# A linear-attention front and two feed-forward layers on one core: the order of small steps around the query tiles, the loads and the weight conversion is rewritten

## The chip, the cores and the metric

One Trainium2 chip, one core of it. The metric is the device time of one execution in microseconds (us); lower is better. Within the core the program uses TensorE (PE: matrix products and transposes), VectorE (DVE), ScalarE (ACT), GpSimd (POOL), and SyncE (SP), which issues all the transfers from one queue.

## The reference, cut to what matters

```python
def phi(x):                                   # x: q or k, scaled
    h = einsum('bhsd,md->bhsm', x, omega) - sum(x*x, -1)/2
    return exp(h - max(h, -1)) / sqrt(m)
kv  = einsum('bhsm,bhsd->bhmd', k_p, v)       # sums over the sequence
num = einsum('bhsm,bhmd->bhsd', q_p, kv)
den = einsum('bhsm,bhm->bhs', q_p, sum(k_p, 2)) + 1e-6
x = num / den                                 # 2304 tokens x 512
xn = x / sqrt(mean(x*x, -1) + 1e-6) * rms_g
y = (silu(xn @ w_gate) * (xn @ w_val)) @ w_out      # 512 -> 1536 -> 512
h = y @ w_in;  out = (h * cos(h)) @ w_out2          # 512 -> 2048 -> 512
```

Four sequences of 576 positions, 8 heads of 64, 128 features; everything is fp32.

## The kernel before, in words

The 2304 tokens are 18 tiles of 128. Each tile goes through the attention once as a key tile and once as a query tile. The code is issued in the order that is written (`manual_schedule`): every engine runs its own queue in that order, and an instruction that waits holds up all that stands behind it on its engine.

**Slots.** The front of the program is 23 slots (`SLOTS`). Each begins one tile: 18 key tiles, and query tiles 0 to 4 in slots 6, 9, 12, 15 and 22, because the sums of the first sequences are then finished. From slot 6 to slot 18 the pattern repeats every three slots: a query tile, a key tile, a key tile; the text calls this a triple. To begin a tile is `project` (16 products on PE into two PSUM banks, `kp_ps` or `qp_ps`) and `features` (on DVE the maximum over features, `kmx`/`qmx`; on ACT eight exponentials per tile, `ke`/`qe`). A key tile's product with v (`kv_product`) follows one slot later, for which the exponentials must be there.

**A query tile's later steps** (`query_step`) come in the slots after its own: 1 `transposed` and `keep_transposed` (PE transposes; the copies `eT` out of PSUM on DVE and ACT), 2 `sums` (PE, `num_ps`) and `quotients` (DVE), 3 `square` (ACT, sum of squares into `ms`), 4 `root` (`ms` times 1/512 plus epsilon on DVE, then the power -1/2 on POOL) and `norm` (DVE: x times `ms` times gain), 5 `turn` (PE transposes of x, `xT_ps`) and `put` 0 (ACT), 6 `put` 1 (DVE), and the store of a finished block of three tiles.

**Half steps.** The other 13 query tiles run beside the first feed-forward layer: each of its steps is two half steps, for gate and value (`gv_ps`, 12 products of 384 columns each), and a half step does the work of one slot: a new query tile every 2 or 3 half steps. After the product of a half step come the attention's steps and then half of the previous step's output product (`y_ps`, 6 products).

**PSUM.** There are four banks with the tag `w`, taken in turn by `kp_ps`, `qp_ps`, `xT_ps`, and, in the half steps, also by `gv_ps`, `eT_ps` and `num_ps`. A step that takes a bank waits until the step that had it four takings earlier has been read out.

**Weights.** Each of 68 chunks of weights (512 KB as raw fp64 bits) is loaded and turned into two fp32r halves: `W` on ACT, four integer operations on DVE (L153, L155, L157, L160), an add on POOL (L164), a cast on ACT (L170), a subtraction on POOL (L172). `tick(n)` issues the next n of these seven pieces. The load of chunk c+3 waits for the POOL add of chunk c, whose buffer it takes. In the slots `tick(4)` stands at the end of each until nine chunks are done.

**Loads.** `att.load` for the tile two slots ahead is the first thing in a slot (`AHEAD = 2`, three buffers). The v tile of three slots ahead is loaded right behind the `kv_product` that frees its buffer, and waits for it; key loads and weight loads stand in the same SP queue.

Of the kernel before, what the change touches and what calls it, by code (L numbers as in the profile page):

```python
# [38 lines left out]
AF = mybir.ActivationFunctionType  # L39
ALU = mybir.AluOpType  # L40
# [13 lines left out]
def attention_then_ffn(ctx: ExitStack, tc: tile.TileContext, qT, kT, v, omT, wc1, rms_g, wc2, out, B, H, S, D):  # L54
    nc = tc.nc
    M = omT.shape[1]
    DM = H * D
# [48 lines left out]
    quarter = const.tile([P, 1], F32, name="quarter")  # L106
    half_pi = const.tile([P, 1], F32, name="half_pi")
# [6 lines left out]
    class Weights:  # L114
# [26 lines left out]
        def run(self):  # L141

            last = len(self.todo)
            for c in range(3):
                self.load(c)
            yield
            self.exponent(0)
            yield
            for c in range(last + 1):
                if c < last:  # L150
                    w, raw = self.w.pop(c), self.raw.pop(c)
                    f = conv.tile([P, 512], I32, tag="f", name=f"f{c}", bufs=3)
                    nc.vector.tensor_scalar(f, w, 3, None, op0=ALU.logical_shift_left)  # L153
                    yield
                    nc.vector.scalar_tensor_tensor(f, w, SIGN, f, op0=ALU.bitwise_and, op1=ALU.bitwise_or)  # L155
                    yield
                    nc.vector.tensor_scalar(raw[:, :, 1], f, SIGN_AND_EXPONENT, None, op0=ALU.bitwise_and)  # L157
                    yield
                    rest = f32(raw[:, :, 1])
                    nc.vector.scalar_tensor_tensor(rest, raw[:, :, 0].bitcast(U32), 2.0 ** -52, rest,  # L160
                                                   op0=ALU.mult, op1=ALU.mult)
                    self.exponent(c + 1)
                    yield
                    nc.gpsimd.tensor_tensor(f32(f), f32(f), rest, op=ALU.add)  # L164
                    self.f[c] = f32(f)
                    yield
                    self.load(c + 3)
                if c > 0:
                    t = wpool.tile([P, 2, 512], F32R, tag="w", name=f"w{c - 1}")
                    nc.scalar.copy(t[:, 0], self.f[c - 1])  # L170
                    yield
                    nc.gpsimd.tensor_tensor(t[:, 1], self.f.pop(c - 1), f32(t[:, 0]), op=ALU.subtract)  # L172
                    self.out[self.todo[c - 1]] = t
                    self.done = c
                    yield
# [20 lines left out]
    wts = Weights()  # L196


    class Attention:
# [41 lines left out]
        def keep_transposed(self, t, r):  # L241
            ps = self.ps.pop(("eT", t, r))
            eT = self.tile_of("featT", [P, HP, P], F32, f"eT{t}_{r}")
            ps = ps.rearrange("p (h n) -> p h n", h=HP)
            if r or self.tag == "w":
                nc.scalar.copy(eT, ps)
            else:
                nc.vector.tensor_copy(eT, ps)
            self.eT[t, r] = eT
# [28 lines left out]

        def root(self, t):
            ms = self.ms[t]  # L280
            nc.vector.tensor_scalar(ms, ms, 1.0 / DM, 1e-6, op0=ALU.mult, op1=ALU.add)
            nc.gpsimd.tensor_tensor(ms, ms, minus_half, op=ALU.pow)

        def norm(self, t):
# [37 lines left out]
    with tc.manual_schedule():  # L322
        fp = ctx.enter_context(tc.tile_pool(name="fp", bufs=2, reuse_waits="tile"))
        early = ExitStack()
        ap = early.enter_context(tc.tile_pool(name="att", bufs=2, side="right", reuse_waits="tile"))
        depth = {"gain": 1, "raw": 3, "feat": 6, "mx": 6, "den": 4}
        kv = [ap.tile([P, KVW], F32, name=f"kv{b}", bufs=1) for b in range(B)]
        NV = 3
        vt = [ap.tile([P, H + 1, D], F32, name=f"v{i}", bufs=1) for i in range(NV)]
# [6 lines left out]
        def load_v(t):  # L336
            if t < NTILE:
                nc.sync.dma_start(vt[t % NV][:, 0:H], v[t])

        def kv_product(t, i):  # L340

            b, p0, n = parts(t)[i]
            end = p0 + n + t * P == (b + 1) * S
            for r in range(2):
                begin = (b, r) not in acc
                if begin:
                    acc[b, r] = bank("kv", f"kv_ps{b}_{r}")
                for h in range(HP):
                    hh = 2 * h + r
                    nc.tensor.matmul(  # L350
                        acc[b, r][:, h * P:(h + 1) * P], att.e["k", t, r][p0:p0 + n, h, :],
                        vt[t % NV][p0:p0 + n, hh::H - hh, :],
                        start=begin and h == 0, stop=end, skip_group_check=True)
                if end:
                    keep_kv(b, r)
            if i == len(parts(t)) - 1:
                for r in range(2):
                    del att.e["k", t, r]
                load_v(t + NV)

        def keep_kv(b, r):
            nc.vector.tensor_copy(
# [4 lines left out]
        def query_step(t, s):  # L367

            if s == 1:
                for r in range(2):  # L370
                    att.transposed(t, r)
                    att.keep_transposed(t, r)
            elif s == 2:
                for r in range(2):
                    att.sums(t, r)
                    att.quotients(t, r)
            elif s == 3:
                att.square(t)
            elif s == 4:
                att.root(t)  # L380
                att.norm(t)
            elif s == 5:
                att.turn(t)
                att.put(t, 0)
            elif s == 6:
                att.put(t, 1)
                if t % TPB == TPB - 1:
                    store(t // TPB, "x")
# [3 lines left out]
        tiles = {s: ("k", s) for s in range(6)}  # L392
# [3 lines left out]
        SLOTS = len(tiles)  # L396
# [3 lines left out]
        begins, then = {}, {}  # L400
        for s, (nm, t) in tiles.items():
            if nm == "k":
                for i in range(len(parts(t))):
                    then.setdefault(s + 1 + i, []).append((1, kv_product, t, i))
            else:
                for i in range(1, 7):
                    then.setdefault(s + i, []).append((-i, query_step, t, i))
        for todo in then.values():
            todo.sort(key=lambda e: e[0])
        AHEAD = 2  # L410
        order = sorted(tiles)

        def slot_before(s):

            at = order.index(s) if s in tiles else -1
            if at >= 0 and at + AHEAD < len(order):
                att.load(*tiles[order[at + AHEAD]])
            for k, f, *args in then.get(s, []):
                if k in (-6, -4):
                    f(*args)  # L420

        def slot_after(s):
            if s in tiles:
                att.project(*tiles[s])
                for r in range(2):
                    att.features(*tiles[s], r)
            for k, f, *args in then.get(s, []):
                if k not in (-6, -4):
                    f(*args)

        nc.sync.dma_start(om, omT)
        att.load(*tiles[0])
        att.load(*tiles[1])
        load_v(0)
        wts.tick(1)
        load_v(1)
        load_v(2)
        att.load_gain()
        for a in vt:
            nc.vector.memset(a[:, H], 1.0)  # L440
        for a in kv:
            nc.vector.memset(a[:, H * (D + 1):], 0.0)
        make_identity(nc, ident)
        nc.gpsimd.memset(quarter, 0.25)
        nc.gpsimd.memset(half_pi, math.pi / 2)
        nc.gpsimd.memset(minus_half, -0.5)
        nc.vector.tensor_scalar(om, om, SCALE, None, op0=ALU.mult)

        UP = 9
        for s in range(SLOTS):  # L450
            slot_before(s)
            slot_after(s)
            if wts.done < UP:
                wts.tick(4)


        att.tag = "w"
# [178 lines left out]
        for n, (g, blk, f, first, last) in enumerate(steps):  # L636
            in_g = len(GROUPS1[g]) * NBLK
            left = in_g - n % in_g - 3
            rate = rate_of(C1 * NF1 // 3 * (g + 2), left) if left > 0 else 0
            if g == 0 and n < G:  # L640
                rate = max(rate, 8)
            if n % in_g == 0:
                wts.freed = C1 * len(GROUPS1[0]) * g
            s = SLOTS + 2 * n
            slot_before(s)
            ps = product(blk, f, 0)
            a = silu(blk, f, ps)
            slot_after(s)
            if n >= 1:
                out1(*steps[n - 1][:3], hid[n - 1], *steps[n - 1][3:], (0, 1))  # L650
            wts.pace(rate / 2)
            flush(3)
            slot_before(s + 1)
            ps = product(blk, f, 1)
            hid[n] = gated(blk, f, a, ps)
            slot_after(s + 1)
            if n >= 1:
                out1(*steps[n - 1][:3], hid.pop(n - 1), *steps[n - 1][3:], (2, 3))
            if n in fetches:
                fetch(fetches[n], f"xhl{g}_{fetches[n]}")  # L660
            if g == 1 and f == GROUPS1[1][1]:
                take_back(blk)
            wts.pace(rate / 2)
            flush(3)
# [83 lines left out]
```

## Time and profile before

| | us |
|---|---|
| median of 3 runs (1034.16 to 1036.82) | 1035.8 |
| the profiled execution | 1034.51 |
| its span, first to last instruction | 1032.7 |
| PE busy in the span | 1001.7 (97%) |
| DVE busy | 630.3 (61%) |
| ACT busy | 474.8 (46%) |
| POOL busy | 191.9 (19%) |

PE is busy for 97% of the span, so what can be won is where it is not, and where it runs at its lower clock. A busy share over the whole span says nothing on a stage: the rows below are cut by stage. Times are from the start of the span. A line "[idle before <-releaser]" gives how long that engine had been idle ahead of the instruction and whose end ended it.

### The profile page before, as it was taken

Reading aid. Unit: us, or ns where it says so; the run is one execution under the profiler, and the core shown is the slowest. Engines: PE = TensorE matmul, PEld = TensorE weight load, DVE = VectorE, ACT = ScalarE, POOL = GpSimd, SP = SyncE. Lnnn points to the kernel's source line nnn. Section 1 sums busy time; section 2 is a strip of 40 time slices with the busy share of each in tenths; the row PEclk is TensorE's granted clock in tenths of the full one; section 3 lists DMA queues with packets and bytes.
Section 4 is the critical chain, followed back from the end, with each engine's and each line's share of the span. In section 5 each row is a group of like instructions: output and inputs, shape, how many; then the busy total and the mean of one; then the engine's idle time right before and its main releaser. Section 6 shows DMA issues by size and latency. Waiting matters only on the chain.

```text
span 1032.7 us, 15416 instructions
## 1 busy us (share of the span) xinstructions
PE 1001.7 (97%) x6040; PEld 948.0 (92%) x6040; DVE 630.3 (61%) x1180; ACT 474.8 (46%) x1018; POOL 191.9 (19%) x163
## 2 busy tenths in 40 slices
PE   7979899999999999999999999999999999999998
PEld 6878898998999999999999999878999999999997
DVE  5876575655524555324666337988667777566655
ACT  5766766856722222212333224555545444434443
POOL 1431222221101332102333001333112221000000
PEclk8998999999999999999999999999999999999999
DMA  7545142422221643502455412335202341003401
GB/s 247 205 153 175 63 159 77 163 94 81 112 93 50 246 153 126 190 1 88 160 181 209 158 62 82 123 134 192 82 21 103 121 179 67 2 1 123 153 31 61
DMA packets 32616, 121.90 MB, mean 118 GB/s; under 512 B 3616, under 2 KB 9888, under 8 KB 27936
## 3 DMA queue, kind: packets, MB, share of 16 engines
q1 hardware_dynamic: 32544, 120.93, 32.7%
q8 instruction: 47, 0.77, 0.3%
q14 instruction: 25, 0.20, 0.1%
HBM read 92.60 MB, written 28.31 MB: 117 GB/s over the span
## 4 chain that ended last, share of the span: by engine, by line
PE 72%; DVE 3%; ACT 1%; issue 0%; POOL 0%
PE gv_ps L462 8%; PE gv_ps L461 8%; PE gv_ps L463 8%; PE o_ps L463 6%; PE h_ps L463 6%; PE h_ps L461 6%; PE h_ps L462 6%; PE o_ps L462 6%; PE o_ps L461 6%; PE y_ps L461 4%; PE y_ps L462 4%; PE y_ps L463 4%; PE num_ps L258 1%; DVE o L574 1%; DVE turns L564 0%
## 5 line engine op out<-in xcount | busy, mean ns | idle before, releaser
L461 PE MATMUL gv_ps<-xhl,w 128*128 128x384 f32 x576 | 192.8, 335 | 1.8 <-DVE den L268 1.8
L463 PE MATMUL gv_ps<-xhl,w 128*128 128x384 f32 x576 | 192.6, 334 | 0.0
L462 PE MATMUL gv_ps<-xhl,w 128*128 128x384 f32 x576 | 192.4, 334 | 0.0
L164 POOL TENSOR_TENSOR f<-f,raw 128x512 f32<-128x512 f32 x68 | 90.2, 1326 | 530.9 <-issue 304.2
L463 PE MATMUL h_ps<-yhl,w 128*128 128x384 f32 x384 | 129.5, 337 | 0.0
L461 PE MATMUL h_ps<-yhl,w 128*128 128x384 f32 x384 | 129.3, 337 | 0.0
L462 PE MATMUL h_ps<-yhl,w 128*128 128x384 f32 x384 | 129.0, 336 | 0.0
L526 DVE TENSOR_TENSOR gv<-gv_ps,gv 128x384 f32<-128x384 f32 x72 | 40.1, 557 | 141.6 <-PE gv_ps L463 134.7
L527 ACT CAST t<-gv 128x384 fp32r<-128x384 f32 x72 | 37.0, 513 | 193.6 <-DVE gv L526 193.6
L463 PE MATMUL o_ps<-w,o 128*128 128x512 f32 x288 | 114.4, 397 | 0.6 <-DVE o L574 0.4
L462 PE MATMUL o_ps<-w,o 128*128 128x512 f32 x288 | 113.7, 395 | 0.0
L461 PE MATMUL o_ps<-w,o 128*128 128x512 f32 x288 | 112.4, 390 | 1.0 <-DVE osum L584 0.6
L569 ACT ACTIVATE turns<-turns,half_pi 128x384 f32<-128x384 f32 x96 | 59.3, 617 | 114.6 <-DVE turns L564 114.6
L461 PEld LDWEIGHTS gv_ps<-xhl,w 128*128 128x128 f32 x576 | 108.1, 188 | 2.4 <-issue 1.2
L462 PEld LDWEIGHTS gv_ps<-xhl,w 128*128 128x128 f32 x576 | 108.1, 188 | 0.0
L463 PEld LDWEIGHTS gv_ps<-xhl,w 128*128 128x128 f32 x576 | 108.1, 188 | 0.0
L172 POOL TENSOR_TENSOR w<-f,w 128x512 fp32r<-128x512 f32 x68 | 92.2, 1356 | 79.0 <-ACT w L170 49.2
L461 PE MATMUL y_ps<-t,w 128*128 128x384 f32 x288 | 99.5, 345 | 0.0
L463 PE MATMUL y_ps<-t,w 128*128 128x384 f32 x288 | 96.4, 335 | 0.0
L462 PE MATMUL y_ps<-t,w 128*128 128x384 f32 x288 | 96.4, 335 | 0.0
L574 DVE TENSOR_TENSOR o<-turns,o 128x384 fp32r<-128x384 f32 x96 | 61.4, 639 | 47.0 <-ACT o L572 47.0
L572 ACT CAST o<-turns 128x384 fp32r<-128x384 f32 x96 | 49.3, 514 | 75.5 <-DVE turns L571 74.5
(72 smaller groups left out, 1771.7 us busy)
## 6 DMA issues: line engine op xcount, KB each, us to landing
raw<-wc SPq DMA_DIRECT2D x68, 512.0 KB, 3.6
yhl<-y_dram SPq DMA_DIRECT2D x14, 1536.0 KB, 6.9
xhl<-x_dram SPq DMA_DIRECT2D x10, 1536.0 KB, 8.2
x_dram<-xhl SPq DMA_DIRECT2D x6, 1536.0 KB, 5.1
y_dram<-yhl SPq DMA_DIRECT2D x6, 1536.0 KB, 7.3
kraw<-kT SPq DMA_DIRECT2D x18, 256.0 KB, 3.8
v<-v SPq DMA_DIRECT2D x18, 256.0 KB, 3.0
qraw<-qT SPq DMA_DIRECT2D x18, 256.0 KB, 3.7
```

What stands on the lines that cost most here:

```text
L164: nc.gpsimd.tensor_tensor(f32(f), f32(f), rest, op=ALU.add)
L172: nc.gpsimd.tensor_tensor(t[:, 1], self.f.pop(c - 1), f32(t[:, 0]), op=ALU.subtract)
L258: nc.tensor.matmul(ps[p0:p0 + n, h * P:(h + 1) * P], eT[:, h, p0:p0 + n], self.kv[b][:, at:at + P], start=True, stop=True, skip_group_chec ...
L461: nc.tensor.matmul(o, w[0], x[0], start=first, stop=False)
L462: nc.tensor.matmul(o, w[0], x[1], start=False, stop=False)
L463: nc.tensor.matmul(o, w[1], x[0], start=False, stop=last)
L526: nc.vector.tensor_tensor(a, ps, a, op=ALU.mult)
L527: nc.scalar.copy(t[:, 0], a)
L569: nc.scalar.activation(r, r, AF.Sin, bias=half_pi)
L572: nc.scalar.copy(o[:, 0], r)
L574: nc.vector.tensor_tensor(o[:, 1], r, f32(o[:, 0]), op=ALU.subtract)
```

## The change

- `root`'s first operation goes from DVE to POOL, so both are on POOL. `root` is issued behind the slot's own tile, and `norm` is a step of its own at the start of the next slot; `turn` stays in that slot, behind `project`.
- Loads go three tiles ahead with four buffers (`AHEAD = 3`); the `feat` buffers are five instead of six. At the start the third key tile is loaded ahead of all weights, chunks 0 to 2 one by one in slots 0 to 2, the gain in slot 3. The v load goes to the start of the slot after the `kv_product` that frees it.
- The pieces of conversion per slot are none in slot 0, 5 in slots 1 to 5, 2 in slots 6 to 17 (where there are query tiles) and 4 in slots 18 to 22, instead of 4 in each until nine chunks are done.
- In a half step the older query tiles come first: `norm` ahead of all, then after the product `turn`, `root`, `square`, `sums`, `put` 1, then the new tile, the output product, and last the transposes of features.
- One of a tile's two `eT` copies is on DVE in the half steps too (14 tiles; it was ACT).
- An exponential of one column is issued at the start (it brings ACT's table load there).

```diff
-            for c in range(3):
-                self.load(c)
-            yield
...
-            if r or self.tag == "w":
+            if r:
...
-            nc.vector.tensor_scalar(ms, ms, 1.0 / DM, 1e-6, op0=ALU.mult, op1=ALU.add)
+            nc.gpsimd.tensor_scalar(ms, ms, 1.0 / DM, 1e-6, op0=ALU.mult, op1=ALU.add)
...
-        depth = {"gain": 1, "raw": 3, "feat": 6, "mx": 6, "den": 4}
+        depth = {"gain": 1, "raw": 4, "feat": 5, "mx": 6, "den": 4}
...
-                load_v(t + NV)
...
+            elif s == 5:
                 att.norm(t)
-            elif s == 5:
+            elif s == 6:
                 att.turn(t)
                 att.put(t, 0)
-            elif s == 6:
+            elif s == 7:
                 att.put(t, 1)
...
+                then.setdefault(s + 2 + i, []).append((0, load_v, t + NV))
...
-                for i in range(1, 7):
-                    then.setdefault(s + i, []).append((-i, query_step, t, i))
+                for i in range(1, 8):
+                    late = s + i - (i > 5) - (i == 7 and s + i > SLOTS + 1)
+                    then.setdefault(late, []).append((-i, query_step, t, i))
...
-        AHEAD = 2
+        AHEAD = 3
...
+        att.load(*tiles[2])
+        wts.load(0)
+        nc.gpsimd.memset(quarter, 0.25)
+        nc.scalar.activation(half_pi, quarter, AF.Exp)
...
-            slot_before(s)
-            slot_after(s)
-            if wts.done < UP:
-                wts.tick(4)
+            load_ahead(s)
+            if s in (0, 1):
+                load_v(s + 1)
+                wts.load(s + 1)
+            if s == 3:
+                att.load_gain()
+            older(s, 0, -7, -5)
+            begin(s)
+            older(s, -6, -4, -3, -2, -1, 1)
+            if s:
+                wts.tick(5 if s < 6 else 2 if s < 18 else 4)
...
-            slot_before(s)
+            load_ahead(s)
+            older(s, -5)
             ps = product(blk, f, 0)
             a = silu(blk, f, ps)
-            slot_after(s)
+            older(s, -6, -4, -3, -2, -7)
+            begin(s)
             if n >= 1:
                 out1(*steps[n - 1][:3], hid[n - 1], *steps[n - 1][3:], (0, 1))
+            older(s, -1, 1, 0)
             wts.pace(rate / 2)
```

Three places show how instructions move. First SP's queue near the start of the program, from the first v tile on. Before:

```order
L338 DMA v_89<-v 128x512
L132 DMA raw_98<-wc 128x1024
L132 DMA raw_100<-wc 128x1024
L132 DMA raw_102<-wc 128x1024
L338 DMA v_90<-v 128x512
L338 DMA v_91<-v 128x512
L290 DMA gain<-rms_g 128x512
L210 DMA kraw_123<-kT 128x512
```

And now:

```order
L335 DMA v_89<-v 128x512
L207 DMA kraw_98<-kT 128x512
L132 DMA raw_100<-wc 128x1024
L207 DMA kraw_118<-kT 128x512
L335 DMA v_90<-v 128x512
L132 DMA raw_121<-wc 128x1024
```

The third key tile stood behind three chunks of weights, two v tiles and the gain (2304 KB); now nothing stands between it and the first v tile.

Second, DVE's queue in the third triple (slots 12 and 13 of the text above: query tile 2 and the key tile after it). Before:

```order
L229 TENSOR_REDUCE qmx_0_715<-qp_ps_0_704 128x4
L229 TENSOR_REDUCE qmx_1_722<-qp_ps_1_705 128x4
L153 TENSOR_SCALAR f_742<-W_693 128x512
L155 SCALAR_TENSOR_TENSOR f_742<-W_693,f_742 128x512
L157 TENSOR_SCALAR raw_526<-f_742 128x512
L160 SCALAR_TENSOR_TENSOR raw_526<-raw_526 128x512
L281 TENSOR_SCALAR ms_729<-ms_729 128x1
L286 SCALAR_TENSOR_TENSOR x_667<-x_667,ms_729,gain 128x512
L229 TENSOR_REDUCE kmx_0_765<-kp_ps_0_754 128x4
L229 TENSOR_REDUCE kmx_1_772<-kp_ps_1_755 128x4
L248 COPY eT_0_783<-eT_ps_0_778 128x512
```

And now:

```order
L226 TENSOR_REDUCE qmx_0_696<-qp_ps_0_685 128x4
L226 TENSOR_REDUCE qmx_1_703<-qp_ps_1_686 128x4
L157 SCALAR_TENSOR_TENSOR raw_326<-raw_326 128x512
L226 TENSOR_REDUCE kmx_0_740<-kp_ps_0_729 128x4
L226 TENSOR_REDUCE kmx_1_747<-kp_ps_1_730 128x4
L245 COPY eT_0_760<-eT_ps_0_755 128x512
L283 SCALAR_TENSOR_TENSOR x_655<-x_655,ms_710,gain 128x512
L226 TENSOR_REDUCE kmx_0_788<-kp_ps_0_777 128x4
```

`ms` and the norm of x stood ahead of the key tile's maxima; now one conversion piece does, and the norm stands behind these maxima and the `eT` copy, ahead of the next key tile's.

Third, PE's queue in a half step that has a `turn`, `sums` and a new query tile, from behind the half step's product. Before:

```order
L220 MATMUL qp_ps_0_1885<-om,qraw_1582 128x128
L220 MATMUL qp_ps_1_1886<-om,qraw_1582 128x128
L296 MATMUL xT_ps_1909<-ident,x_1722 128x128 x4
L258 MATMUL num_ps_0_1915<-kv_86,eT_0_1841 128x128 x4
L258 MATMUL num_ps_1_1925<-kv_86,eT_1_1848 128x128 x4
L461 MATMUL y_ps_1_0_2_1852<-t_0_1769,w_421 128x384
```

And now:

```order
L466 MATMUL gv_ps_1_1_1865<-xhl_1128,w_771 128x384
L293 MATMUL xT_ps_1882<-ident,x_1719 128x128 x4
L255 MATMUL num_ps_0_1888<-kv_86,eT_0_1849 128x128 x4
L255 MATMUL num_ps_1_1898<-kv_86,eT_1_1856 128x128 x4
L217 MATMUL qp_ps_0_1908<-om,qraw_1394 128x128
L217 MATMUL qp_ps_1_1909<-om,qraw_1394 128x128
```

The new tile's projection went from ahead of `turn` and `sums` to behind them. On DVE the same place, from the half step before it. Before:

```order
L229 TENSOR_REDUCE qmx_1_1791<-qp_ps_1_1774 128x4
L157 TENSOR_SCALAR raw_1519<-f_1742 128x512
L160 SCALAR_TENSOR_TENSOR raw_1519<-raw_1519 128x512
L490 COPY y_3_1814<-y_ps_0_0_3_1383 128x384
L281 TENSOR_SCALAR ms_1798<-ms_1798 128x1
L286 SCALAR_TENSOR_TENSOR x_1722<-x_1722,ms_1798,gain 128x512
L526 TENSOR_TENSOR gv_1_1834<-gv_ps_1_1_1868,gv_1_1834 128x384
L528 TENSOR_TENSOR t_1_1881<-gv_1_1834,t_1_1881 128x384
```

And now:

```order
L493 COPY y_3_1813<-y_ps_0_0_3_1367 128x384
L245 COPY eT_0_1849<-eT_ps_0_1844 128x512
L154 TENSOR_SCALAR raw_1523<-f_1806 128x512
L157 SCALAR_TENSOR_TENSOR raw_1523<-raw_1523 128x512
L283 SCALAR_TENSOR_TENSOR x_1719<-x_1719,ms_1773,gain 128x512
L529 TENSOR_TENSOR gv_1_1830<-gv_ps_1_1_1865,gv_1_1830 128x384
```

The norm is one half step later than it was (its tile's `turn` is in the same half step now), and ahead of it, behind the `eT` copy, stand two pieces of conversion.

## Rows read from the trace of the kernel before

**Rows 1.** Windows: length; busy PE, PEld, DVE, ACT, POOL (instructions); PE clock, DMA share, GB/s.
```profile
0.00:28.00 28.00, 21.02 (x174) 19.73 (x175) 14.79 (x33) 15.77 (x49) 6.22 (x14) 0.88 0.69 237
...
40.50:85.90 45.40, 35.94 (x327) 33.20 (x326) 34.95 (x72) 30.15 (x96) 16.05 (x14) 0.89 0.47 157
85.90:102.70 16.80, 16.80 (x181) 15.95 (x181) 9.89 (x18) 10.71 (x39) 0.55 (x1) 1.00 0.68 220
102.70:300.00 197.30, 188.43 (x1360) 180.94 (x1359) 112.64 (x250) 130.75 (x281) 41.10 (x40) 1.00 0.30 106
```

**Rows 2.** Waits of PE up to 110 us: total, times, longest.
```profile
PE kp_ps L220 <- DMA kraw<-kT: 8.5, 3, 3.8
PE xT_ps L296 <- ACT ke L231: 7.9, 3, 3.7
```

**Rows 3.** Timeline of PE near the start: start, length, instructions.
```profile
13.54 2.08 PE L220 MATMUL kp_ps<-om,kraw 64*128 64x128 f32 x16 [3.14 <-DMA kraw<-kT]
15.56 3.78 PE L350 MATMUL kv_ps<-v,ke 128*128 128x128 f32 x16
...
20.45 2.05 PE L350 MATMUL kv_ps<-v,ke 128*128 128x128 f32 x16
```

**Rows 4.** Timeline of PE: where query tiles 1 and 2 begin.
```profile
40.48 1.16 PE L220 MATMUL qp_ps<-om,qraw 64*128 64x128 f32 x16
...
53.14 1.16 PE L220 MATMUL qp_ps<-om,qraw 64*128 64x128 f32 x16
```

**Rows 5.** Timeline of PE in the third triple.
```profile
73.47 1.09 PE L238 MATMUL eT_ps<-ident,qe 128*128 128x128 f32 x8
...
79.31 1.12 PE L296 MATMUL xT_ps<-ident,x 128*128 128x128 f32 x4 [3.65 <-ACT ke L231]
80.22 3.62 PE L258 MATMUL num_ps<-kv,eT 128*128 128x128 f32 x16
```

**Rows 6.** Timeline of DVE in the third triple.
```profile
71.96 0.42 DVE L153 TENSOR_SCALAR f<-W 128x512 int32<-128x512 int32 x1
72.41 0.69 DVE L155 SCALAR_TENSOR_TENSOR f<-W,f 128x512 int32<-128x512 int32 x1
74.30 0.15 DVE L281 TENSOR_SCALAR ms<-ms 128x1 f32<-128x1 f32 x1 [1.20 <-ACT sq L277]
76.66 0.75 DVE L286 SCALAR_TENSOR_TENSOR x<-x,ms,gain 128x512 f32<-128x512 f32 x1 [2.21 <-POOL ms L282]
77.33 1.28 DVE L229 TENSOR_REDUCE kmx<-kp_ps 128x4 f32<-128x512 f32 x2
78.53 0.68 DVE L248 COPY eT<-eT_ps 128x512 f32<-128x512 f32 x1
```

**Rows 7.** Source lines: duration in ns, least/median/most, of all 18.
```profile
L286 DVE SCALAR_TENSOR_TENSOR x<-x,ms,gain x18: 750/753/1793, 46.1 to 288.5; 128x512 f32<-128x512 f32 x18
L282 POOL TENSOR_TENSOR ms<-ms,minus_half x18: 544/549/558, 45.5 to 288.0; 128x1 f32<-128x1 f32 x18
```

**Rows 8.** Groups by line up to 110 us: the key tiles' exponentials.
```profile
L231 ACT ACTIVATE ke<-kp_ps,kmx 128x128 f32<-128x128 f32 x144 | 39.4, 394 | 28.1 <-DVE kmx L229 28.1
```

**Rows 9.** Waits from 103 to 300 us: total, times, longest.
```profile
DVE x L286 <- POOL ms L282: 17.6, 14, 3.2
...
DVE ms L281 <- ACT sq L277: 13.2, 9, 2.7
...
PE num_ps L258 <- DVE x L270: 5.1, 3, 2.2
```

**Rows 10.** Timelines of POOL, DVE and PE around one half step.
```profile
156.72 1.31 POOL L164 TENSOR_TENSOR f<-f,raw 128x512 f32<-128x512 f32 x1
...
156.79 1.79 DVE L286 SCALAR_TENSOR_TENSOR x<-x,ms,gain 128x512 f32<-128x512 f32 x1 [0.66 <-POOL ms L282]
...
163.98 1.13 PE L258 MATMUL num_ps<-kv,eT 128*128 128x128 f32 x8 [2.16 <-DVE x L270]
```

**Rows 11.** Window of products of 384 columns without a pause.
```profile
300.00:400.00 100.00, 100.00 (x579) 100.00 (x578) 47.01 (x83) 27.56 (x54) 23.57 (x18) 1.00 0.37 135
```

More of the change, by code (lines that the diff above doesn't have):

```diff
@@ L404, in attention_then_ffn, with load_ahead @@
                     then.setdefault(s + 1 + i, []).append((1, kv_product, t, i))
+                then.setdefault(s + 2 + i, []).append((0, load_v, t + NV))
             else:
-                for i in range(1, 7):
-                    then.setdefault(s + i, []).append((-i, query_step, t, i))
+                for i in range(1, 8):
+                    late = s + i - (i > 5) - (i == 7 and s + i > SLOTS + 1)
+                    then.setdefault(late, []).append((-i, query_step, t, i))
         for todo in then.values():
             todo.sort(key=lambda e: e[0])
-        AHEAD = 2
+        AHEAD = 3
         order = sorted(tiles)
-        def slot_before(s):
+        def load_ahead(s):
             at = order.index(s) if s in tiles else -1
@@ L417, in slot_before, with older, begin @@
                 att.load(*tiles[order[at + AHEAD]])
[L418 to L422, printed above, removed]
+        def older(s, *steps):
+            for step in steps:
+                for k, f, *args in then.get(s, []):
+                    if k == step:
+                        f(*args)
+        def begin(s):
             if s in tiles:
@@ L426, in slot_after @@
                     att.features(*tiles[s], r)
-            for k, f, *args in then.get(s, []):
-                if k not in (-6, -4):
-                    f(*args)
         nc.sync.dma_start(om, omT)
@@ L434, in attention_then_ffn @@
         load_v(0)
[L435 to L438, printed above, removed]
+        att.load(*tiles[2])
+        wts.load(0)
+        nc.gpsimd.memset(quarter, 0.25)
+        nc.scalar.activation(half_pi, quarter, AF.Exp)
         for a in vt:
@@ L443, in attention_then_ffn @@
         make_identity(nc, ident)
-        nc.gpsimd.memset(quarter, 0.25)
         nc.gpsimd.memset(half_pi, math.pi / 2)
@@ L447, in attention_then_ffn @@
         nc.vector.tensor_scalar(om, om, SCALE, None, op0=ALU.mult)
-        UP = 9
         for s in range(SLOTS):
-            slot_before(s)
-            slot_after(s)
-            if wts.done < UP:
-                wts.tick(4)
+            load_ahead(s)
[9 more added lines that the diff above has]
+                wts.tick(5 if s < 6 else 2 if s < 18 else 4)
         att.tag = "w"
@@ L644, in attention_then_ffn @@
             s = SLOTS + 2 * n
-            slot_before(s)
+            load_ahead(s)
+            older(s, -5)
             ps = product(blk, f, 0)
             a = silu(blk, f, ps)
-            slot_after(s)
+            older(s, -6, -4, -3, -2, -7)
+            begin(s)
             if n >= 1:
                 out1(*steps[n - 1][:3], hid[n - 1], *steps[n - 1][3:], (0, 1))
+            older(s, -1, 1, 0)
             wts.pace(rate / 2)
             flush(3)
-            slot_before(s + 1)
+            load_ahead(s + 1)
+            older(s + 1, -5)
             ps = product(blk, f, 1)
             hid[n] = gated(blk, f, a, ps)
-            slot_after(s + 1)
+            older(s + 1, -6, -4, -3, -2, -7)
+            begin(s + 1)
             if n >= 1:
                 out1(*steps[n - 1][:3], hid.pop(n - 1), *steps[n - 1][3:], (2, 3))
+            older(s + 1, -1, 1, 0)
             if n in fetches:
```

## The prediction

> **What bounds the kernel now.** I read the windows by stage first. PE has no rival: from 102.7 us on it is busy almost throughout, and in the page's sums no other engine passes 61%. What can be won is PE's idle time and its slow clock, and these lie in three stretches [rows 1]. Up to 28 us PE is busy 21.02 us, with a mean granted clock of 0.88; from 40.50 to 85.90, three triples of slots, 35.94 of 45.40 us, at 0.89; from 102.70 to 300, the half steps with query tiles, 188.43 of 197.30, at full clock. From 85.90 to 102.70 there is nothing to win: 16.80 of 16.80.
>
> Next, who ends these waits. In the slots PE waits 8.5 us for key loads and 7.9 us at `turn` for exponentials of a key tile [rows 2]; 3.8 of the 8.5 are the first load, which nothing here moves. The waits at `turn` need to be followed one engine further. In the third triple `turn` waits 3.65 us [rows 5] for a bank that ACT's exponentials must first read out; these need the maxima `kmx`, and `kmx` begins on DVE only at 77.33, because `ms` and the norm stand ahead of it and wait 1.20 us for ACT's sum of squares and 2.21 us for POOL's power [rows 6]. PE's fault is DVE's queue. In the half steps DVE spends 17.6 and 13.2 us in the same two waits, and of PE's 8.87 us idle (197.30 - 188.43) 5.1 are `sums` waiting for a bank that DVE's quotients free [rows 9]. Rows 10 show one of these: the norm ends at 158.58, all behind it is late, and `sums` waits 2.16 us.
>
> The slow clock follows the gaps. Behind the 3.14 us wait for the third key tile the same 16 products of a `kv_product` take 3.78 us, against 2.05 later [rows 3]; behind the 3.65 us at `turn` the 16 `num_ps` products take 3.62 [rows 5], where 8 take 1.13 at full clock [rows 10]. These are the levels 1.2 and 2.4 GHz.
>
> **The change part by part; gains are negative.**
>
> *Start.* The third key tile's load stood behind 3136 KB, now behind 832 (sizes from the tiles' shapes). It landed by 13.54 us [rows 3]; in proportion to the KB with its own 256, 13.54 x 1088/3392 gives 4 us, before PE asks at 10.40. So the wait of 3.14 goes, and with it, I take it, the slow products: 2.08 - 1.16 for the projection [rows 3, 4] and 3.78 - 2.05 for `kv_product`, 2.65 together: 5.8 at most. A new wait comes: chunk 0's four pieces on DVE now stand ahead of the third tile's maxima, and need `W`, which stands on ACT behind two tiles' exponentials (39.4/144 x 8 = 2.2 us a tile [rows 8]). Walking the queues on from the second tile's exponentials (ending near 10.9): `W` 11.5, four pieces of 0.42 or 0.69 (two like the rows shown [rows 6]) until 13.8, maxima of half a tile 14.4, first exponentials 15.5; PE would want them at 14.7, so it waits 0.8, and about half of that again at each of the next two tiles. I take 1.7 us. Start: -4.1, between -5.8 and 0 (the load late anyway, or the clock no better).
>
> *Triples.* `ms` and the norm leave the place ahead of `kmx`. Two loads that came late (1.6 us of the 8.5 [rows 2] lies here: 8.5 less 3.8 and 3.1) have a slot more. PE's own work in 45.40 us is 35.94, less what the slow clock added: which I take as 3.5 (3.62 to 2.26 in the third triple's `num_ps`, some tenths in its neighbours, about as much in the second triple), 32.4, or 10.8 a triple. Now the norm stands right ahead of its `turn`. From the start of the first key tile of a triple: projection 1.16, transposes about 0.9, second projection 1.16: PE is at `turn` at 3.2. DVE: maxima until 2.45, `eT` copy 0.68 until 3.1, none or one piece of 0.42, norm 0.75 [rows 6, 7]: 3.9 to 4.3. The wait is 0.7 to 1.1, I take 0.8: 11.6 a triple, 34.8 for three, -10.6. Bounds: -13.0 with no wait, -7.3 if all triples take 12.66 as the first did (40.48 to 53.14 [rows 4]), which had neither a late load nor slow products.
>
> *Less conversion per triple* (6 pieces for 12) is paid later: about 20 pieces, nearly three chunks, move into 85.90 to 102.70. DVE had 9.89 us of 16.80 [rows 1]; three chunks at 2.2 bring it to about 16.3, almost full, so PE will wait now and then: +1.5, between 0 and +3.
>
> *Half steps.* The 30.8 us of DVE waits for roots and sums of squares go, and with the older tiles first the banks of `sums` are ones freed a half step before. I count all 8.87 us as removed. Against it stands the norm ahead of `turn`. In 8 of 13 cases the half step before ends in transposes; from their end PE has the 12 products of the next half step, 12 x 100/579 = 2.1 us [rows 11], while DVE does the `eT` copy, two or three pieces of conversion (1.1 to 1.5), sometimes a copy of `y`, and the norm: 2.3 to 3.4, less what of the copy overlaps the last transposes. Wait: 0.15 to 1.3, I take 0.6, so 8 x 0.6 = 4.8, and none for the other five. Half steps: -4.1, between -8.9 and +1.5.
>
> *At nothing:* POOL's new operation on one column, bounded by the power's 0.55 us [rows 7] and nothing; I take 0.5, 18 x 0.5 = 9 us, hidden since POOL works 16.05 of 45.40 us and the norm comes a slot later. Without that slot it would add its 0.5 to each. The `eT` copies on DVE: 14 x 0.68, inside DVE's 112.64 of 197.30, counted above where they precede a norm. The exponential at the start: ACT is idle until the first maxima. Five `feat` buffers: query tile 0's second exponentials wait for half of a `kv_product`, whose slot has 3.8 us of other PE work. The v load a slot start later still has two slots.
>
> The Trainium skill warns against this move: Perfetto Trace Analysis, Optimizing Scalar/DVE Operations, says VectorE and GpSimd share an SBUF port, "so offloading operations between those two might not help". The rows agree that the two meet: a norm took 1.79 us beside a POOL add [rows 10], against a median of 0.753 [rows 7]; by that rule the sum would have the second rival's time.
>
> **Sum:** -4.1 - 10.6 + 1.5 - 4.1 = -17.3. The profiled execution took 1034.51 us (span 1032.7), so 1017.2; the median of the runs lies 1.3 higher, 1035.8: **1018.5**.
>
> **Rivals.**
>
> *The exponentials are the chain anyway* (18%). The wait is booked on ACT, and the first triple, with no late load, took 12.66. For: ACT has 30.15 us in the three triples, 10 each. Against: half of its conversion goes. Then the triples give -7.3, the half steps perhaps -2: -4.1 - 7.3 + 1.5 - 2 = -11.9, 1023.9.
>
> *Each norm beside a POOL piece* (10%): 1.04 us more (1.79 less 0.75) at 3 triples and 8 half steps, +11.4: 1029.9. For: conversion's POOL pieces are now free to fall anywhere. Against: the most is 1.793 and the median 0.753.
> The page SBUF — State Buffer of the Trainium skill, Who interferes with whom, has the two block each other for a whole instruction; the 1.79 agrees, and how often it falls on a norm only a run tells.
>
> *The root is still late* (6%), so that the change doesn't do what it says: POOL's root stands behind an add of 1.31 [rows 10]. With 0.5 + 0.55 that is 2.4 us, under a slot. If not, only start and late loads are won, -4.1 - 1.6: 1030.1.
>
> *Slower: the norm lands behind whole conversions* (8%). Without any wait at `turn` the sum is -5.8 + 1.7 - 13.0 + 1.5 - 8.9 = -24.5. There are 3 + 13 turns, so it decides at 1.53 us each. Four pieces (2.2) with copy and norm (1.43) need 3.65 against 2.1: just that. At 2.0 each: +7.5, 1043.3. Against: the order shows two or three pieces in front of the norm.
>
> **Numbers.** My forecast has 58%. A measurement of this kernel tells about 0.3% (3 us). The range 1011 to 1029 takes in the first rival, the bounds of start and triples in part, and leaves out the last three cases and the floor (1035.8 - 5.8 - 13.0 - 8.9 = 1008): about 2 in 10. The forecast's own range is 1012 to 1024. Faster by over 0.3%: 58 + 18 and most of the second and third rivals, less a little for what I have not seen, 86%; within 0.3%: 6%; slower: 8%.
>
> **What would show it.** Right: no wait for a key load behind the first; granted clock 1.00 from about 8 us on; no `ms` on DVE and no wait of DVE for POOL; three triples in 33 to 37 us; the first `gv_ps` product near 90 us; `sums` without waits for quotients; short waits at `turn`, ended by the norm. Wrong: if `turn`'s waits pass 1.5 us, if norms take 1.8, or if the slots from 18 on stretch by more than 3 us.

## The result, and the profile after

| | before | changed |
|---|---|---|
| median, us | 1035.12 (4 runs) | 1023.91 (4 runs, 1023.42 to 1024.06) |
| profiled execution, its span | 1034.51, 1032.7 | 1024.06, 1022.3 |
| first `gv_ps` product (the half steps begin) | 102.72 | 89.80 |
| from there to the end of the span | 929.98 | 932.50 |

The ratio is 0.9889, with an interval of 0.9872 to 0.9906: 11.2 us faster, where 17.3 were forecast. The table has the reason in two lines: the slots gave 12.9 us, against 13.2 in the forecast's sum; the half steps gave nothing and lost 2.5, where 4.1 were to be won.

The windows by stage of the changed kernel (columns as in [rows 1]), cut where the same work stands:

```profile
0.00:24.00 24.00, 19.59 (x183) 18.41 (x185) 15.33 (x32) 15.30 (x48) 5.26 (x13) 1.00 0.78 275
...
36.00:71.00 35.00, 31.07 (x321) 28.56 (x320) 28.02 (x56) 27.00 (x93) 9.84 (x12) 1.00 0.46 148
71.00:90.00 19.00, 18.67 (x196) 17.66 (x195) 15.89 (x30) 13.44 (x45) 6.37 (x6) 1.00 0.72 258
90.00:290.00 200.00, 190.44 (x1354) 182.14 (x1353) 122.66 (x255) 126.53 (x269) 50.82 (x56) 0.99 0.31 106
```

In the slots the granted clock is 1.00 throughout, where it was 0.88 and 0.89. In the half steps PE's idle time is 9.56 of 200 us, as much as before (8.87 of 197.30), and the clock is no longer full there. Who ends PE's waits in the changed kernel, first up to 100 us, then from 90 to 300 (total, times, longest):

```profile
PE xT_ps L293 <- DVE x L283: 4.3, 4, 1.7
PE kp_ps L217 <- DMA kraw<-kT: 4.1, 1, 4.1
```

```profile
PE xT_ps L293 <- DVE x L283: 8.3, 7, 2.7
PE gv_ps L464 <- DVE den L265: 1.0, 1, 1.0
```

Of the key loads only the first is waited for. `sums` no longer wait for quotients. In their place stands one wait, the transposes of x for the norm: 12.6 us in 11 of 18 turns. The timeline of PE at the start and in the triples shows the rest (start, length, instruction):

```profile
10.79 1.16 PE L217 MATMUL kp_ps<-om,kraw 64*128 64x128 f32 x16
11.88 2.05 PE L347 MATMUL kv_ps<-v,ke 128*128 128x128 f32 x16
...
23.51 0.37 PE L217 MATMUL qp_ps<-om,qraw 64*128 64x128 f32 x1
...
37.00 1.16 PE L217 MATMUL qp_ps<-om,qraw 64*128 64x128 f32 x16
...
45.08 0.63 PE L293 MATMUL xT_ps<-ident,x 128*128 128x128 f32 x4 [1.73 <-DVE x L283]
...
49.21 1.16 PE L217 MATMUL qp_ps<-om,qraw 64*128 64x128 f32 x16
...
60.87 1.16 PE L217 MATMUL qp_ps<-om,qraw 64*128 64x128 f32 x16
...
72.57 1.16 PE L217 MATMUL kp_ps<-om,kraw 64*128 64x128 f32 x16
```

The third key tile begins at 10.79 instead of 13.54, and its products and those behind it run at the full level (1.16 and 2.05 against 2.08 and 3.78 [rows 3]). The three triples take 12.21, 11.66 and 11.70 us.

And one turn of the half steps, the worst: DVE, then PE.

```profile
130.22 1.33 DVE L531 TENSOR_TENSOR t<-gv,t 128x384 fp32r<-128x384 f32 x1 [1.23 <-ACT t L530]
131.47 0.68 DVE L245 COPY eT<-eT_ps 128x512 f32<-128x512 f32 x1
132.07 0.41 DVE L150 TENSOR_SCALAR f<-W 128x512 int32<-128x512 int32 x1
132.52 0.69 DVE L152 SCALAR_TENSOR_TENSOR f<-W,f 128x512 int32<-128x512 int32 x1
133.24 0.43 DVE L154 TENSOR_SCALAR raw<-f 128x512 int32<-128x512 int32 x1
133.71 0.69 DVE L157 SCALAR_TENSOR_TENSOR raw<-raw 128x512 f32<-128x512 uint32 x1
134.31 0.74 DVE L283 SCALAR_TENSOR_TENSOR x<-x,ms,gain 128x512 f32<-128x512 f32 x1
```

```profile
135.12 0.66 PE L293 MATMUL xT_ps<-ident,x 128*128 128x128 f32 x4 [2.69 <-DVE x L283]
135.61 3.06 PE L255 MATMUL num_ps<-kv,eT 128*128 128x128 f32 x16
```

The norm waits for nothing but its turn on DVE: ahead of it stand the `eT` copy and a whole chunk's four pieces. Behind the wait PE is slow: the mean granted clock from 130 to 140 us is 0.83, and from 136 to 140 it is 0.57, for the most part at the lower of its two levels.

### The profile page after: what moved, and what is told of

Its sections match the earlier page's. It is cut to its first block, busy times and chain, and to the rows that moved or that the text cites. A ratio compares the mean times of both kernels' runs of the same rounds, so it can differ in the third digit from the quotient of the medians.

```text
span 1022.3 us, 15407 instructions
## 1 busy us (share of the span) xinstructions
PE 999.1 (98%) x6040; PEld 944.5 (92%) x6040; DVE 637.0 (62%) x1176; ACT 469.2 (46%) x1005; POOL 199.2 (19%) x181
## 4 chain that ended last, share of the span: by engine, by line
PE 79%; DVE 11%; ACT 6%; issue 2%; POOL 1%; DMA 1%; SPq 0%; DVEq 0%; POOLq 0%
PE gv_ps L464 9%; PE gv_ps L465 9%; PE gv_ps L466 9%; PE h_ps L466 6%; PE h_ps L464 5%; PE h_ps L465 5%; PE o_ps L465 5%; PE o_ps L466 5%; PE o_ps L464 5%; PE y_ps L464 5%; PE y_ps L466 4%; PE y_ps L465 4%; PE num_ps L255 2%; PE kv_ps L347 2%; ACT qe L228 2%
## 5 line engine op out<-in xcount | busy, mean ns | idle before, releaser
L161 POOL TENSOR_TENSOR f<-f,raw 128x512 f32<-128x512 f32 x68 | 92.3, 1358 | 524.1 <-issue 206.4
L577 DVE TENSOR_TENSOR o<-turns,o 128x384 fp32r<-128x384 f32 x96 | 58.7, 611 | 43.8 <-ACT o L575 43.8
L524 ACT ACTIVATE gv<-gv_ps 128x384 f32<-128x384 f32 x72 | 35.4, 492 | 106.0 <-PE gv_ps L466 105.8
```

The source lines that it names most:

```text
L524: nc.scalar.activation(a, ps, AF.Silu)
L577: nc.vector.tensor_tensor(o[:, 1], r, f32(o[:, 0]), op=ALU.subtract)
```

## The experiments

Theory: the slots won by the loads at the start, by the norm's place behind the key tile's maxima, and by fewer pieces of conversion in a triple; the half steps lost at `turn`, because of what stands ahead of the norm on DVE. Rivals: another part did it, or the wait only moves on. All runs are timed in three rounds beside the kernel before; a ratio is to that kernel in the same rounds, and the changed kernel's is 0.9889.

**The half steps as they were.** For query tiles from 4 on: root on DVE, root and norm one step ahead of turn, new tile ahead of turn and sums, copies on ACT.

```diff
-            if r:
+            if r or self.tag == "w":
...
-            older(s, -5)
+            older(s, -7, -4, -5)
...
-            older(s, -6, -4, -3, -2, -7)
             begin(s)
+            older(s, -6, -3, -2, -1, 1, 0)
...
-            older(s, -1, 1, 0)
...
```

> Half steps in the order of before (root on DVE, norm in the step before turn, new tile ahead of turn and sums, all eT copies on ACT), the slots as in the change. Theory: the change won its time in the slots (first gv_ps product at 89.80 against 102.72) and lost 2.5 us in the half steps, from 929.98 to 932.50 us. Then this starts the half steps near 90 and needs 930 from there: a span of 1019.8, 1021.5 us, 2.4 below the changed kernel; the waits of PE at num_ps for DVE's quotients are back (5 us) and those at xT_ps for the norm are gone. Rival: the new order does help the half steps, and what they lost is the later conversion; then this is slower than the changed kernel, 1026 or more.

Measured: 1019.62 us, ratio 0.9845 (0.9828 to 0.9862). Half steps begin at 90.09 and take 927.9 us (1018.0 - 90.09). PE's waits from 88 to 300 us:

```profile
PE num_ps L255 <- DVE x L267: 4.0, 3, 1.6
PE gv_ps L464 <- DVE den L265: 1.5, 1, 1.5
PE xT_ps L293 <- DVE gv L529: 0.9, 2, 0.5
PE num_ps L255 <- ACT eT L243: 0.7, 2, 0.4
```

The theory holds: what the change did to the half steps cost about 4.3 us, in these waits' place. But this run puts back two things together, the order and the place of the `eT` copies, and the copies alone give back 3.9 us (two runs further on). So the loss is not shown to come from the order by itself; no run has the old order with a copy left on DVE. The time is 2 us better than I had it; why the old half steps need 927.9 here and 929.98 before is open.

**The norm earlier.** The norm for the next half step's turn goes to the end of the half step before, ahead of `eT` and the conversion.

```diff
-            older(s, -5)
             ps = product(blk, f, 0)
...
+            older(s + 1, -5)
             older(s, -1, 1, 0)
             wts.pace(rate / 2)
...
```

> The changed kernel with the norm of the next half step's turn issued at the end of the half step before, ahead of the eT copy and the conversion pieces, instead of behind them. Theory: PE's 8.3 us at xT_ps in the half steps come from what stands ahead of the norm on DVE, and the slow clock near 135 us follows the longest of them; both go: 8 to 10 us less, 1014 to 1016 us, with DVE's waits at eT (19.5 us) shorter and a few us of new waits of DVE for POOL's root. Rival: the wait moves on: the norm now waits for POOL's root, the eT copy behind it is late, and sums wait for eT: 1022 to 1026.

Measured: 1017.26 us, 0.9823 (0.9807 to 0.984). The same turn on DVE and PE:

```profile
130.69 0.75 DVE L283 SCALAR_TENSOR_TENSOR x<-x,ms,gain 128x512 f32<-128x512 f32 x1 [0.72 <-POOL ms L279]
131.35 0.69 DVE L245 COPY eT<-eT_ps 128x512 f32<-128x512 f32 x1
```

```profile
131.49 0.66 PE L293 MATMUL xT_ps<-ident,x 128*128 128x128 f32 x4 [0.63 <-DVE x L283]
132.19 2.02 PE L255 MATMUL num_ps<-kv,eT 128*128 128x128 f32 x16
```

DVE waits 0.72 us for the root, which stands on POOL behind a subtraction of conversion up to 129.56. The `eT` copy behind the norm is held up by it, for its transposes were done by 128.8, but PE does not wait for that copy here. `turn` waits 0.63 us instead of 2.69, the 16 `num_ps` products take 2.02 instead of 3.06, and the mean granted clock of the window 130 to 140 is 1.00. Of the waits at `turn` for the norm one is left, 0.6 us, and there is a new one of 1.0 us for an `eT` copy. From the first product the half steps take 925.7 us (1015.5 - 89.80), 4.3 less than before the change. The gain is 6.7 us, a little under the 8 to 10 expected: 4.1 of the 210.2 us behind the first product are still idle on PE.

**The copies on ACT.** Both `eT` copies of a half step's tile on ACT, as before the change.

```diff
-            if r:
+            if r or self.tag == "w":
                 nc.scalar.copy(eT, ps)
```

> The changed kernel with both eT copies of a half step's tile on ACT, as before the change. Theory: the copy of 0.68 us stands ahead of the norm in the seven turns that wait (8.3 us in all), so these shrink by up to 4.8 us: 1019 to 1021 us. Rival: DVE's copy runs while PE still transposes the second half and adds little, and ACT with two copies is later with them than DVE was: 1023 to 1026, with sums waiting for eT on ACT.

Measured: 1020.01 us, 0.9847 (0.9829 to 0.9865). PE's waits from 88 to 300 us begin with:

```profile
PE xT_ps L293 <- DVE x L283: 4.3, 6, 2.1
```

At `turn` the waits for the norm went from 8.3 to 4.3 us, and the granted clock from 130 to 140 us is 1.00. The copy does stand in the way; ACT has room for it (PE waits 1.0 us in all for its copies). The half steps take 927.8 us (1017.4 - 89.63), 4.7 less than in the changed kernel and 2.2 less than before the change: one copy on DVE was enough to turn the half steps from a win into a loss.

**The old loads at the start.** Weights, two v tiles and the gain ahead of the third key tile.

```diff
+        for c in range(3):
+            wts.load(c)
+        load_v(1)
+        load_v(2)
+        att.load_gain()
         att.load(*tiles[2])
-        wts.load(0)
...
-            if s in (0, 1):
-                load_v(s + 1)
-                wts.load(s + 1)
-            if s == 3:
-                att.load_gain()
```

> The changed kernel with the start's loads in the old order: three chunks of weights, two v tiles and the gain ahead of the third key tile. Theory: the wait of 3.1 us for that tile and the slow products behind it are back, less the new wait at the third tile's maxima: 3 to 6 us more, 1027 to 1030, with a mean granted clock up to 24 us near 0.88 as before. Rival: most of the start's gain comes from no conversion in slot 0, and the load is hidden: within 1 us of 1024.

Measured: 1028.27 us, 0.9928 (0.9909 to 0.9946): 4.4 us more than the changed kernel. PE:

```profile
14.72 1.83 PE L217 MATMUL kp_ps<-om,kraw 64*128 64x128 f32 x16 [4.70 <-DMA kraw<-kT]
16.48 2.97 PE L347 MATMUL kv_ps<-v,ke 128*128 128x128 f32 x16
```

The wait is back and the products behind it are slow, as forecast, if less so: the mean granted clock up to 24 us is 0.93, where I expected 0.88.

**The old conversion in the slots.** Four pieces a slot from slot 6 until nine chunks are done.

```diff
-            if s:
-                wts.tick(5 if s < 6 else 2 if s < 18 else 4)
+            if s and wts.done < 9:
+                wts.tick(5 if s < 6 else 4)
```

> The changed kernel with four pieces of conversion in each slot from 6 on until nine chunks are done, instead of two up to slot 17 and four after. Theory: a triple has about 11.7 us against 10.8 of PE's own work because the norm stands ahead of turn on a DVE that is not full; with six pieces more a triple (3.3 us of DVE) the norm is later and the waits at turn grow by 0.7 to 1.5 us each in three triples, while slots 18 to 22 get their 0.3 us back: 1026 to 1028 us. Rival: DVE has that time to spare and the pieces are hidden: within 1 us of 1024.

Measured: 1028.1 us, 0.9935 (0.9917 to 0.9953), 4.2 more. One turn carries most of it, that of the first triple:

```profile
47.05 1.09 PE L293 MATMUL xT_ps<-ident,x 128*128 128x128 f32 x4 [3.83 <-DVE x L283]
```

It waits 3.83 us instead of 1.73, and behind it PE runs at the lower level (granted clock 0.50 from 46 to 52 us); that triple takes 16.9 us (36.87 to 53.81). The second and third take 12.3 and 11.7, so the cost is spread less evenly than I expected.

**Root and norm together at the old place**, in the slots alone, both operations of root on GpSimd.

```diff
...
-            older(s, 0, -7, -5)
+            older(s, 0, -7, -4, -5)
             begin(s)
-            older(s, -6, -4, -3, -2, -1, 1)
+            older(s, -6, -3, -2, -1, 1)
```

> The changed kernel with root (both operations on GpSimd) and norm together at the head of the slot before turn, as before the change, for the tiles of the slots; half steps as in the change. Theory: the norm stands ahead of the key tile's maxima again and DVE waits there for ACT's sum of squares and POOL; turn then waits for exponentials: triples of 12.5 to 13 us against 11.7, so 2.5 to 4 us more, 1026 to 1028. Rival: with the loads early and half the conversion, ACT is done sooner and the place of the norm costs nothing: within 1 us of 1024, or less since turn no longer waits for the norm.

Measured: 1033.23 us (1029.93 to 1035.37, 10 runs), 0.9983 (0.9968 to 0.9997): 9.3 us more, nearly all that the change had won. DVE, then PE's waits up to 96 us:

```profile
42.88 1.75 DVE L283 SCALAR_TENSOR_TENSOR x<-x,ms,gain 128x512 f32<-128x512 f32 x1 [3.23 <-POOL ms L279]
44.55 1.27 DVE L226 TENSOR_REDUCE kmx<-kp_ps 128x4 f32<-128x512 f32 x2
```

```profile
PE xT_ps L293 <- ACT ke L228: 10.3, 4, 3.1
```

The chain of [rows 5, 6] is back: DVE waits, `kmx` begins late, and the bank that `turn` wants is read late. I had expected 2.5 to 4 us; the triples take 13.8, 13.6 and 13.7, which is 5.5 more for the three, and one more such wait of 1.57 us follows them. The ten runs spread over 5.4 us, with mean clocks from 0.993 to 1.000, where the changed kernel's four lie within 0.64. In the profiled run, one of the faster (1031.61), the granted clock is 1.00 from 36 to 78 us, behind three of these waits; where the slower runs lose up to 3.8 us more is not shown, as they left no trace.

**Loads two ahead** (`AHEAD = 2`, three buffers), the start as changed.

```diff
-        depth = {"gain": 1, "raw": 4, "feat": 5, "mx": 6, "den": 4}
+        depth = {"gain": 1, "raw": 3, "feat": 5, "mx": 6, "den": 4}
...
-        AHEAD = 3
+        AHEAD = 2
...
-            load_ahead(s)
+            if s:
+                load_ahead(s)
```

> The changed kernel with loads two tiles ahead and three buffers, the start's order unchanged. Theory: only the 1.6 us of late loads in the triples can come back, as less conversion leaves SP's queue freer: 1024 to 1026. Rival: the third tile ahead is what keeps keys from standing behind weight loads that wait for POOL, and each late key also slows the clock: 1028 or more.

Measured: 1023.3 us, 0.9885 (0.9866 to 0.9903): the same. The third tile ahead is worth nothing here; key loads are waited for 4.8 us instead of 4.1 up to 88 us, of which 4.0 are the first, so the depth had little part in making them late.

**Root's first operation on DVE**, at its new place.

```diff
-            nc.gpsimd.tensor_scalar(ms, ms, 1.0 / DM, 1e-6, op0=ALU.mult, op1=ALU.add)
+            nc.vector.tensor_scalar(ms, ms, 1.0 / DM, 1e-6, op0=ALU.mult, op1=ALU.add)
```

> The changed kernel with the first operation of root back on DVE, at the new place in the order. Theory: the win in the slots comes from the norm's new place (undoing it cost 9 us), not from the engine of the small operation, whose input is there by then: 1023 to 1025.5, with a few us of DVE waits for ACT's sum of squares that delay nothing. Rival: DVE stops at it for ACT in each of 18 tiles, with kmx, quotients and eT behind it, and GpSimd was what freed it: 1028 or more.

Measured: 1026.52 us, 0.9923 (0.9904 to 0.9942), 2.6 more: between the two, and at the edge of the noise, for this interval just touches that of the changed kernel (0.9872 to 0.9906). DVE never stands idle for ACT ahead of it, but the turns' waits grow a little, to 9.1 us in 10 turns from 90 to 300, where they were 8.3 in 7. The profiled spans differ by only 1.6 us, and where the rest is I did not find.

**The norm earlier in the slots too.**

```diff
-            older(s, 0, -7, -5)
+            older(s, 0, -7)
             begin(s)
-            older(s, -6, -4, -3, -2, -1, 1)
+            older(s, -6, -4, -3, -2)
+            older(s + 1, -5)
+            older(s, -1, 1)
```

> The norm at the end of the step before, ahead of the eT copies and the conversion, in the half steps (as in norm_early, 1017.3) and in the slots too. Theory: the 4.3 us at turn in the slots shrink to 1 or 2: 1014 to 1015.5. Rival: in the slots the sum of squares ends late on ACT, behind a tile's exponentials, so that the norm waits for POOL's root there and delays the eT copy, and sums wait instead: 1017 to 1019.

Measured: 1017.58 us, 0.983 (0.9813 to 0.9848): no more than in the half steps alone. The waits at `turn` in the slots went from 4.3 to 3.5 us only; DVE now waits there 2.3 us for the root, and POOL, ahead of the root, 9.2 us in three tiles for ACT's sum of squares. The first half of the rival's mechanism was right, the sum of squares is late; the second, `sums` waiting for `eT`, did not come (0.5 us, where it was 0.6).

**Both: the norm earlier and the copies on ACT.**

> norm_early (1017.3) with both eT copies of the half steps on ACT too (alone 3.9 less than the changed kernel). Theory: both take away the same wait at turn, of which norm_early has left about 1 us, so they don't add: 1016 to 1018. Rival: the copies also free DVE for gated products and quotients, and they add: 1014 or less.

Measured: 1015.75 us, 0.9823 (0.9801 to 0.9845): against the kernel before it is the same ratio as the early norm alone, so they don't add. The three versions with the early norm are the best kernels here.

## Why the prediction was right, and where it was not

| term | forecast | measured |
|---|---|---|
| start, to slot 6 | -4.1 | -4.6 (28.07 to 23.51) |
| slots 6 to 8 | 0 | +1.1 (12.41 to 13.49 us) |
| three triples | -10.6 | -9.8 (45.4 to 35.57) |
| slots 18 to 22 | +1.5 | +0.4 (16.86 to 17.23) |
| half steps and what follows | -4.1 | +2.5 (929.98 to 932.50) |
| sum | -17.3 | -10.4 |

The measured terms are from the two profiled executions; the medians differ by 11.2 us.

*Start.* The load, its wait and the clock went as worked out, and the experiment with the old loads gave back 4.4 us. The new wait for the third tile's maxima, put at 1.7 us, was too large: PE's only booked wait for exponentials is 0.2. The exponential at the start moved nothing that shows: ACT's table load of 1.28 us begins at 0.73 us before and 0.71 now. Slots 6 to 8 were counted as unchanged; they are 1.1 us longer, with a 0.56 us wait of `sums` for an `eT` copy (0.32 before) among it, and I did not look further. That the slots' sum agrees to 0.3 us is in part luck: this miss is made up for by slots 18 to 22, which lost 1.1 less than forecast.

*Triples.* Right: the norm's place made the difference (9.3 us when undone, 5.5 of it in the triples of the profiled run), fewer pieces of conversion helped (4.2), and the new wait for the norm is 1.73, 0.99 and 1.22 us, the sum 3.9 where 2.4 was taken. The parts undone one by one, with the start's 4.4, make 17.9 us and the slots gave only 12.9: they overlap, and how is not shown.

*Loads three ahead* were given credit for 1.6 us of late loads. That was wrong in its cause: with two ahead only 0.8 us of such waits is back, and the time is the same.

*Half steps.* This is the step that failed: the term of the norm ahead of `turn`, with the `eT` copies on DVE at nothing beside it. "8 x 0.6 = 4.8" is 8.3 in seven turns, 1.2 each. I had counted two or three pieces of conversion ahead of the norm; at 130 us there were four, as in the rival "the norm lands behind whole conversions", though not at every turn. The copies, put at nothing but for their part in that wait, cost 4.7 us of the half steps, by the run that put them back on ACT. The prediction's own sign of being wrong, a wait at `turn` above 1.5 us, came twice: 1.73 in the first triple, 2.69 here. "All 8.87 us as removed" was nearly so: PE's idle time from the first product on is 14.23 us before and 13.85 now, and without the 8.3 at `turn` it would be 8.7 less than before. And nothing was put in for the clock: PE is busy 2.9 us more for the same work (915.75 before, 918.65 now). The granted clock of 0.57 from 136 to 140 us makes about 1.7 of that, by my estimate (0.43 of 4 us); the rest is open, and most of it is there in the early norm's trace too (917.38). In short, -8.7 + 8.3 + 2.9 = +2.5 in place of -8.9 + 4.8 = -4.1.

That the norm's place made the loss is shown by the early norm: with the waits for it gone, the half steps take 6.8 us less than in the changed kernel and 4.3 less than before. That this is close to the -4.1 of the forecast is chance: with no wait for the norm the forecast's own terms give -8.9. Other waits are left or new, such as those for quotients and for an `eT` copy.

*The rivals.* The time, 1023.9, is also the first rival's, but not by its mechanism (and 3 x 12.66 from 45.40 is -7.4, not -7.3, so that its sum is 1023.8): the triples did not stay at 12.66, and `turn` waits for the norm, not for exponentials. The second, the norm beside a POOL piece each time, did not come: 18 norms take 0.745 us in the median, 1.352 at most. So the warning in the Trainium skill (Perfetto Trace Analysis, Optimizing Scalar/DVE Operations) does not decide here: with the small operation on GpSimd the kernel was 2.6 us faster, at the edge of the noise, and what part of that is the engine's is open. The lock that the Trainium skill describes (SBUF — State Buffer, Who interferes with whom) does show, in two of the rows above: the 1.33 us of `t` at 130.22, against 0.56 for the same operation at 143.48, stands beside a POOL subtraction from 129.85 on, and in the run with root and norm at the old place the norm of 1.75 us at 42.88 beside one from 42.81 on.

## What to carry to other kernels

An operation that waits for two other engines costs what stands behind it in its queue, not its own time; move it to where its queue would wait anyway, and then look at what now stands ahead of it. When a step is placed right ahead of its reader, count the filler work in between at its most, not at its mean: the one turn with four pieces ahead of the norm had the longest wait, and slow products behind it. And look at each place that an operation can have by itself: one copy on DVE cost 4 us, which an experiment that undid it together with the order would have put down to the order. A wait on PE can be paid twice, the second time in slow products, as that of 2.69 us was; but this can't be told from its length alone, for the waits of 2.73, 2.94 and 3.07 us with root and norm at the old place had full clock behind them.

## What the runs showed of the hardware that was not expected

- The scaling of one column on GpSimd takes 0.193 us in the median (0.190 at least), against 0.144 on DVE in the run that had it there; I had taken 0.5.
- PE's clock fell behind a wait of 2.69 us in one kernel (0.57 over 136 to 140 us), and stayed at 1.00 behind waits of 2.73, 2.94 and 3.07 us in the profiled run of another. Ten runs of that other kernel had mean clocks from 0.993 to 1.000 and times 5.4 us apart.
